# A third head's scores moved ahead of the value product, one split sum of two lanes, and two tile chains put around a value sum

## The chip, the cores and the metric

The kernel runs on one core of one Trainium2 chip. The metric is the device time of the run in microseconds, the median of several runs. Engines are named as in the profile: PE multiplies matrices (PEld is its weight load), DVE, ACT and POOL work on vectors, SP issues DMAs; POOL and ACT can issue DMAs too.

## The reference

A gated mix of two branches over the same x (2048 rows of 512): attention with 32 heads of 16 within a sliding window of 256, and a SwiGLU network with 1792 hidden columns.

```python
def _A_ref(x, wqkv, wo):
    B, S, D = x.shape
    H = 32; Dh = D // H; W = 256
    ...
    scores = jnp.einsum("bhqd,bhkd->bhqk", q, k) * (Dh ** -0.5)
    mask = (idx[:, None] - idx[None, :] >= 0) & (idx[:, None] - idx[None, :] < W)
    p = _softmax(jnp.where(mask[None, None], scores, -1e9), axis=-1)
    o = jnp.einsum("bhqk,bhkd->bhqd", p, v)
    return (lambda x, *d: x.transpose(*d))(o, 0, 2, 1, 3).reshape(B, S, D) @ wo
def _B_ref(x, w_gate, w_up, w_down):
    return (_silu(x @ w_gate) * (x @ w_up)) @ w_down
g = _sigmoid((x * gate_w).sum(-1, keepdims=True))
return g * _A_ref(x, A_wqkv, A_wo) + (1 - g) * _B_ref(x, B_w_gate, B_w_up, B_w_down)
```

## The kernel before

All of it is one program written out by hand: the order of the Python calls is the order of each engine's queue. There are three stages: a prologue (values, queries and keys, up to about 165 us), the attention stage (to about 637 us), and the network's second half with the output projections.

Matrices are split into a high and a low half of reduced precision (`split`), so that one product is three matmuls. In the attention stage most of the gate and up products of the network, one *sum* for each of 24 weights (`UNITS`) and four blocks of 512 rows, are made beside the attention. A sum has 3 x 4 = 12 products of 128 rows. The first weight's four sums are made with all 128 rows (`whole`); the others by `lanes`: each product is cut into its lower 64 rows (lane 0) and its upper 64 rows (lane 1). The two halves of the array work side by side, each on its own matmul. Both lanes add into one PSUM bank, so lane 1 must not begin a sum before lane 0 has ended it: it runs `LAG` = 18 steps behind, and its first matmul has a dependence on a later instruction of DVE or ACT (`BEHIND`). One `yield` of `lanes` is one *step*, a matmul of each lane. In the first 18 steps only lane 0 works, in the last 18 only lane 1.

The attention goes by groups of four heads (8 groups, `G`) and blocks of 128 rows (16). One *slot* t is one block of one group, and has four quarters (`hd`), of one head each. In a quarter the queue of PE gets:
- `stage1` (line 562): the scores of the next group's block, of whose masked maximum DVE takes care (line 564). They lie in a ring of three banks.
- `stage2` (line 601): the scores of this group with keys as rows; ACT takes the exponential (line 603) into `pt`, POOL masks it (lines 605 and 608). They lie in a ring of two banks (`pd`).
- some steps of `lanes`, by the table `DEAL`.

Heads 0 and 2 lie on the lower half of the rows, 1 and 3 on the upper; `stage2` takes the heads in the order 1, 0, 3, 2, so that the two scores of a quarter lie on opposite halves. In every fourth slot, behind the second quarter's steps, `av` (line 623) makes the value product of the four blocks before it: up to 96 small matmuls into two banks, of which the second is one of `pd`. `evacuate` empties them: ACT copies the second to `ob` (line 634), DVE copies the first (line 640, or adds both at once in the last group, line 636), and POOL sends the sum to `od`.

The last group (slots 112 to 127) has no `stage1`, and `stage2` is called for two heads at a time. Beside it two finished tiles of the network are made (`tile_early`: an exponential on ACT, then on DVE a sum, a reciprocal and two products, and a split), weights are loaded (`wd_early`, `wd_raw`), and the softmax denominators are inverted (`invert`). Functions put in `AT` by `at(k, ...)` and `later(n, ...)` are called at the end of quarter k. In slot 128 the last value product is made; the next stage's loads `got` (line 863) take the memory that the attention gives back.

Of the kernel before, what the change touches and what calls it, by code (L numbers as in the profile page):

```python
# [2 lines left out]

# [6 lines left out]
F32 = mybir.dt.float32  # L10
F32R = mybir.dt.float32r
AF = mybir.ActivationFunctionType
ALU = mybir.AluOpType
# [3 lines left out]
P = 128  # L17
S, D, H, DH, W, F = 2048, 512, 32, 16, 256, 1792
NK = D // P
NB = S // P  # L20
CH = 512
NCH = S // CH
# [11 lines left out]
def gated_mix(ctx, tc, xT, xn, wqk, wv, wo, wgu, wd, gw, out):  # L34
# [4 lines left out]
    nc = tc.nc  # L39
# [3 lines left out]
    dram = ctx.enter_context(tc.tile_pool(name="dram", bufs=1, space=DRAM))  # L43
# [3 lines left out]
    vd = dram.tile([G, P, NB, VW], F32, name="vd")  # L47
    od = dram.tile([G, P, S], F32, name="od")
    raws = dram.tile([NF, 2, NCH, P, CH], F32, name="raws")
    rd = dram.tile([NCH, H, CH], F32, name="rd")  # L50
    xd = [[dram.tile([2, P, 2 * CH], F32, name=f"xd{g}{hf}") for hf in range(2)] for g in range(G)]

# [33 lines left out]
    def run(gen, n=None):  # L86

        while n is None or n > 0:
            if next(gen, run) is run:
                break  # L90
            n = n and n - 1
# [14 lines left out]
    UNITS = [("f", f, i) for f in range(NSF, NF) for i in range(2)]  # L106
# [4 lines left out]
    def bank(n):  # L111
        names = BANKS[n if isinstance(n, str) else ("pa", "pb", "pc", "pd")[n]]
        names.append(names.pop(0))
        return psum.tile([P, CH], F32, name=names[-1])
# [98 lines left out]
    first = [bank(n // 2) for n in range(4)]  # L213
# [18 lines left out]
    def op_sums(raw):  # L232
        a11, a12, a21, a22 = (raw[:, i] for i in range(4))
        s = wide.tile([P, 4, 2 * P], F32, name="s")
        for o, in0, in1, op in ((1, a21, a22, ALU.add), (2, a11, a21, ALU.subtract),
                                (0, s[:, 1], a11, ALU.subtract), (3, a12, s[:, 0], ALU.subtract)):
            nc.vector.tensor_tensor(out=s[:, o], in0=in0, in1=in1, op=op)
        return s.rearrange("p a n -> p (a n)")
# [27 lines left out]
    for b in range(4, NB):  # L266
        ps = bank((b // 4 % 2) * 2 + b % 4 // 2)
# [21 lines left out]
            split(hi, lo, raw, nc.scalar, nc.gpsimd)  # L289
        return halves  # L290

    WKEYS, PEND = list(UNITS), []

    def prefetch():
        if WKEYS:
# [120 lines left out]
    for p in range(NP):  # L416
# [4 lines left out]
        for i, (n, a) in enumerate(order):  # L421
            product(p, n, a)
            if not last:
                if i == 4:
                    OP["a"] = op_a(RW[p + 1])
                if i == 5:
                    sums = op_sums(RW[p + 1])
# [39 lines left out]
    with ExitStack() as A:  # L467
# [4 lines left out]
        def kept():  # L472
            return sm.tile([P, CH], F32, name="ev", bufs=EV)

        BEHIND, AT, NOW = [], {}, [0]
# [3 lines left out]
        def later(n, *fs):  # L479
            AT.setdefault(NOW[0] + n, []).extend(fs)  # L480

        def at(k, *fs):
            AT.setdefault(k, []).extend(fs)
# [8 lines left out]
        def products(key, c):  # L492
            wh, wl = WT[key]
            return [(wt[:, k], xt[c][:, k]) for k in range(NK) for wt, xt in ((wh, xhi), (wh, xlo), (wl, xhi))]

        def copy_out(key, c, ps):
            place = kept()
            queue = nc.gpsimd if key == UNITS[-1] else nc.sync
            later(0, lambda: nc.scalar.copy(place, ps))
            later(3, lambda: queue.dma_start(raws[key[1], key[2], c], place))  # L500
# [7 lines left out]
                        copy_out(key, c, ps)  # L508
                    yield

        LAG = 3 * NK + 6

        def lanes():


            sums = [(key, c) for key in UNITS[1:] for c in range(NCH)]
            ps, turned = {}, {}
            for n in range(len(sums) * 3 * NK + LAG):
                for lane in range(2):
                    o, i = divmod(n - lane * LAG, 3 * NK)  # L520
                    if not 0 <= o < len(sums):
                        continue
                    if not lane and i == 0:
                        ps[o] = bank("pa")
                    w, x = products(*sums[o])[i]
                    r = slice(64 * lane, 64 * lane + 64)
                    mm = nc.tensor.matmul(ps[o], w[r], x[r], start=not lane and i == 0,  # L527
                                          stop=bool(lane) and i == 3 * NK - 1)
                    if lane and i == 0:
                        tc.add_manual_dep(mm.ins, BEHIND[turned.pop(o)].ins.name, SYNC, reason="the other rows are summed")  # L530
                    if i == 3 * NK - 1:
                        if lane:
                            copy_out(*sums[o], ps.pop(o))
                            if sums[o][1] == NCH - 1:
                                later(3, prepare)
                        else:
                            turned[o] = len(BEHIND)
                yield

        def stream():  # L540
# [9 lines left out]
        def stage1(g, qb):  # L550

            hf, b = divmod(qb, NB // 2)
            if b == 0:
                MX[g, hf] = sm.tile([P, 4, NB // 2], F32, name="mx")
            q0, k0 = qb * P, max(0, qb - 2) * P
            n = q0 + P - k0
            for hd in range(4):
                pr, j = divmod(hd, 2)
                r = slice(64 * j, 64 * j + 63)

                ps = bank("pd") if g == 0 and pr else bank("pc")
                nc.tensor.matmul(ps[:, :n], QT[g % 2][pr][r, q0:q0 + P], KT[g % 2][pr][r, k0:k0 + n],  # L562
                                 start=True, stop=True)
                mx = nc.vector.tensor_tensor_reduce(out=ps[:, :n], in0=ps[:, :n], in1=mask[:, 3 * P - n:],  # L564
                                                    scale=1.0, scalar=NEG, op0=ALU.add, op1=ALU.max,
                                                    accum_out=MX[g, hf][:, hd, b:b + 1])
                if g == 0:
                    BEHIND.append(mx)
                yield
# [43 lines left out]
        def av(g, c):  # L613

            AV[g, c] = bank("pc"), bank("pc" if g == G - 1 or g == G - 2 and c == NCH - 1 else "pd")

            orders = [[4 * c + m for m in ms if 4 * c + m >= 0] for ms in ((0, 1, 2, -1, -2, 3), (0, 1, -1, 2, 3, -2))]
            for n, kbs in enumerate(zip(*orders)):
                for j in range(4):
                    for h, (o, kb) in enumerate(zip(HALVES, kbs)):  # L620
                        k0 = kb * P + 64 * h
                        q0, q1 = max(k0, c * CH), min(k0 + W + 64, c * CH + CH)
                        nc.tensor.matmul(AV[g, c][h][32 * j:32 * j + 32, q0 - c * CH:q1 - c * CH],  # L623
                                         VG[4 * g + kb // 4][o, kb % 4, 17 * j:17 * j + 32],
                                         PT[g, kb, j // 2][o, j % 2, q0 - kb * P:q1 - kb * P],
                                         start=n == 0, stop=n == len(orders[0]) - 1, skip_group_check=True)
# [19 lines left out]
        first = chain(*(stage1(0, b) for b in range(NB)))  # L646
# [91 lines left out]
            wd_early(4 * (g7 + 1 + m) + 2, m, m)  # L738
        for n in range(2):
            at(4 * (g7 + 9) + 1 + n, lambda n=n: tile_load(n, RAW_AT[n]))  # L740
        for n, ticks in enumerate(((2, 5, 5, 5, 5, 10), (4, 8, 8, 8, 8, 14))):
            early = tile_early(n)
            for m in ticks:
                at(4 * (g7 + 10) + m, lambda early=early: run(early, 1))
# [10 lines left out]
            spread(4 * (16 * g + 9) + 3, 1, stack(g + 2, 0))  # L755
            spread(4 * (16 * g + 17) + 1, 1, stack(g + 2, 1))

        DEAL = [[[(hd + 1) * n // 4 - hd * n // 4 for hd in range(4)] for n in deal] for deal in ((4, 9, 9, 8), (9, 9, 9, 8))]
        DEAL[0][0] = 1, 2, 1, 0
        for t in range(G * NB + 1):  # L760
            g, i = divmod(t, NB)
            d, part = divmod(t, NSLOT)
            s1 = stage1(g + 1, i) if t < g7 else iter(())
            s2 = stage2(g, i) if t < G * NB else iter(())
            values = part == 0 and t > 0
            for hd in range(4):
                k = NOW[0] = NSLOT * t + hd
                run(s1, 1)
                if t < g7:
                    run(s2, 1)  # L770
                elif hd % 2 == 0:
                    run(s2, 2)
                if t == G * NB and hd == 0:
                    last_tile = tile_silu(2)
                    run(last_tile, 1)
                if t < G * NB:
                    run(steps, DEAL[t >= g7][part][hd])
                if hd == 1 and values:
                    av(*divmod(d - 1, NCH))
                    while UNDER:  # L780
                        UNDER.pop(0)()
                    evacuate(*divmod(d - 1, NCH))
                tick_end()
            if i in (7, 15) and g + 1 < G:
                UNDER.append(lambda g=g, i=i: put_max(g + 1, i // 8))
            if t >= 10 and t % 4 == 2 and t + 6 < G * NB:
                load_v((t + 6) // 4)
# [196 lines left out]
```

## Time and profile before

| | |
|---|---|
| median of 3 runs | 840.9 us (840.44 to 840.92) |
| the profiled execution | 843.89 us, span 842.2 us |
| PE busy | 830.5 us (99%) |
| PEld, DVE, ACT, POOL busy | 83%, 65%, 56%, 47% |
| DMA | 158.91 MB, 189 GB/s on the mean |
| mean granted clock of PE | 0.998 |

The profile is one execution; its time is above the median of the runs. Busy times count a matmul from its start to a modelled end, so that matmuls that overlap on the two halves of the array count once. In the timeline "x2" is two instructions of one group put together; a group in brackets is what ended the idle time before it. `64*128 64x512` is a matmul with 64 rows of weights and 512 columns.

### The profile page before, as it was taken

What the parts mean: (1) busy time and instruction counts of PE and PEld (TensorE: products, weight loads), DVE (VectorE), ACT (ScalarE), POOL (GpSimd) and SP (SyncE); (2) the same over time, 40 slices, a digit from 0 to 9 for tenths busy, and PEclk for the clock granted to TensorE, in tenths of its full rate; (3) what the DMA queues carried; (4) which work ended last, traced back from release to release, by engine and by line L of the source; (5) the groups of instructions that cost most, each with busy time, mean ns of one, the idle gap of its engine ahead of it and who ended that gap; (6) DMA issues with size and microseconds to landing.
All of it is one profiled execution on the core that took longest, in us unless ns stands there. A gap on an engine that the chain in (4) does not pass through costs nothing.

```text
span 842.2 us, 20499 instructions
## 1 busy us (share of the span) xinstructions
PE 830.5 (99%) x7681; PEld 700.5 (83%) x7681; DVE 548.5 (65%) x1424; ACT 471.3 (56%) x955; POOL 398.9 (47%) x713
## 2 busy tenths in 40 slices
PE   9999999999999999999999999999997999999997
PEld 7888888888888888888988888888775888888886
DVE  5675554258787887878878778675473647564652
ACT  7454553212576776766767667666674554434341
POOL 5124441440475665766666666666654115352220
PEclk9999999999999999999999999999999999999999
DMA  8456676484625656456654545533628899878611
GB/s 296 142 174 225 228 263 222 141 273 152 197 94 163 209 177 198 146 181 191 196 188 141 189 156 190 164 107 127 205 99 278 282 248 259 268 217 249 212 51 50
DMA packets 79843, 158.91 MB, mean 189 GB/s; under 512 B 14912, under 2 KB 19392, under 8 KB 79744
## 3 DMA queue, kind: packets, MB, share of 16 engines
q1 hardware_dynamic: 68256, 126.91, 46.7%
q0 software_dynamic: 10912, 29.65, 11.1%
q8 instruction: 60, 0.98, 0.5%
q10 hardware_dynamic: 576, 1.05, 0.4%
q14 instruction: 39, 0.32, 0.1%
HBM read 92.80 MB, written 64.75 MB: 187 GB/s over the span
## 4 chain that ended last, share of the span: by engine, by line
PE 96%; DMA 1%; POOL 1%; SPq 0%; ACT 0%; DVE 0%; issue 0%; DVEq 0%; ACTq 0%
PE pa L527 22%; PE pb L527 11%; PE pd L601 7%; PE pc L623 4%; PE pd L380 4%; PE pb L380 4%; PE pa L380 4%; PE pc L562 4%; PE pd L82 3%; PE pc L81 3%; PE pc L82 3%; PE pc L80 3%; PE pd L81 3%; PE pd L80 3%; PE pd L623 2%; PE pb L623 2%
## 5 line engine op out<-in xcount | busy, mean ns | idle before, releaser
L603 ACT ACTIVATE pt<-pd 128x384 f32<-128x384 f32 (+2 forms) x512 | 231.9, 474 | 50.8 <-PE pc L562 14.2
L564 DVE CUSTOM_DVE_ANT_0 pc<-pc,mask 128x384 f32<-128x384 f32 (+2 forms) x322 | 172.5, 547 | 33.6 <-PE pc L562 15.2
L601 PE MATMUL pd<-q,k 64*128 64x384 f32 (+2 forms) x512 | 175.1, 357 | 0.7 <-ACT ob L634 0.3
L527 PE MATMUL pa<-xlo,wh 64*128 64x512 f32 x496 | 161.8, 396 | 0.0
L527 PE MATMUL pa<-xhi,wl 64*128 64x512 f32 x496 | 160.2, 392 | 0.0
L527 PE MATMUL pa<-xhi,wh 64*128 64x512 f32 x496 | 159.4, 396 | 0.1
L605 POOL TENSOR_SCALAR_AFFINE_SELECT pt<-pt 128x256 f32<-128x256 f32 x256 | 111.5, 436 | 74.5 <-ACT pt L603 70.2
L601 PEld LDWEIGHTS pd<-q,k 64*128 64x128 f32 x512 | 92.5, 184 | 21.1 <-ACT ob L634 9.7
L562 PE MATMUL pc<-k,q 63*128 63x384 f32 (+2 forms) x322 | 105.9, 333 | 0.0
L527 PE MATMUL pb<-xlo,wh 64*128 64x512 f32 x240 | 94.8, 395 | 0.0
L527 PE MATMUL pb<-xhi,wh 64*128 64x512 f32 x240 | 94.6, 394 | 0.0
L527 PE MATMUL pb<-xhi,wl 64*128 64x512 f32 x240 | 94.2, 393 | 0.0
L564 DVE CUSTOM_DVE_ANT_0 pb<-pb,mask 128x384 f32<-128x384 f32 (+2 forms) x158 | 86.7, 549 | 11.0 <-PE pb L562 5.4
L608 POOL TENSOR_SCALAR_AFFINE_SELECT pt<-pt 128x256 f32<-128x256 f32 x224 | 92.4, 412 | 0.0
L527 PEld LDWEIGHTS pa<-xhi,wl 64*128 64x128 f32 x496 | 81.9, 185 | 1.7
L527 PEld LDWEIGHTS pa<-xhi,wh 64*128 64x128 f32 x496 | 79.9, 186 | 3.6 <-ACT pt L603 1.1
L527 PEld LDWEIGHTS pa<-xlo,wh 64*128 64x128 f32 x496 | 80.8, 185 | 1.3
L869 DVE TENSOR_TENSOR sg<-got,sg 128x512 f32<-128x512 f32 x53 | 41.8, 788 | 49.1 <-ACT sg L868 39.6
L564 DVE DVE_READ_ACCUMULATOR2_ANT mx<- 128x1 f32 x512 | 72.5, 142 | 0.0
L562 PEld LDWEIGHTS pc<-k,q 63*128 63x128 f32 x322 | 58.8, 184 | 7.3 <-issue 4.3
L623 PE MATMUL pd<-pt,vg 64*32 64x320 f32 (+4 forms) x1184 | 63.1, 346 | 0.0
L641 POOL TENSOR_TENSOR oe<-oe,ob 128x512 f32<-128x512 f32 (+1 forms) x28 | 35.0, 1251 | 55.0 <-ACT ob L634 50.9
(302 smaller groups left out, 2055.6 us busy)
## 6 DMA issues: line engine op xcount, KB each, us to landing
got<-raws SPq DMA_DIRECT2D x106, 256.0 KB
raws<-ev SPq DMA_DIRECT2D x92, 256.0 KB
q<-xd SPq DMA_DIRECT2D x96, 128.0 KB
k<-xd SPq DMA_DIRECT2D x96, 128.0 KB
xd<-cx SPq DMA_DIRECT2D x16, 512.0 KB
xd<-cy SPq DMA_DIRECT2D x16, 512.0 KB
od<-oe POOLq DMA_DIRECT2D x32, 256.0 KB, 3.2
raw<-wgu SPq DMA_DIRECT2D x24, 256.0 KB
```

The costliest lines, as they stand in the source:

```text
L80: nc.tensor.matmul(ps, lh, rh, start=start and i == 0, stop=False, skip_group_check=skip)
L81: nc.tensor.matmul(ps, lh, rl, start=False, stop=False, skip_group_check=skip)
L82: nc.tensor.matmul(ps, ll, rh, start=False, stop=stop and i == n - 1, skip_group_check=skip)
L380: nc.tensor.matmul(ps, l[:, w], r[:, k], start=n in (1, 2, 5) and k == m == 0, stop=k == 1 and m == 2, skip_group_check=True)
L527: mm = nc.tensor.matmul(ps[o], w[r], x[r], start=not lane and i == 0, stop=bool(lane) and i == 3 * NK - 1)
L562: nc.tensor.matmul(ps[:, :n], QT[g % 2][pr][r, q0:q0 + P], KT[g % 2][pr][r, k0:k0 + n], start=True, stop=True)
L564: mx = nc.vector.tensor_tensor_reduce(out=ps[:, :n], in0=ps[:, :n], in1=mask[:, 3 * P - n:], scale=1.0, scalar=NEG, op0=ALU.add, op1=ALU.m ...
L601: nc.tensor.matmul(ps[:, :n], KT[g % 2][pr][r, k0:k0 + P], QT[g % 2][pr][r, k0:k0 + n], start=True, stop=True)
L603: BEHIND.append(nc.scalar.activation(pt[:, j, :n], ps[:, :n], AF.Exp, scale=SCALE))
L605: nc.gpsimd.affine_select(out=pt[:, :, :P], in_=pt[:, :, :P], pattern=[[0, 2], [1, P]], compare_op=ALU.is_ge, fill=0.0, base=0, channel_mu ...
L608: nc.gpsimd.affine_select(out=pt[:, :, 2 * P:], in_=pt[:, :, 2 * P:], pattern=[[0, 2], [-1, P]], compare_op=ALU.is_ge, fill=0.0, base=-1, ...
L623: nc.tensor.matmul(AV[g, c][h][32 * j:32 * j + 32, q0 - c * CH:q1 - c * CH], VG[4 * g + kb // 4][o, kb % 4, 17 * j:17 * j + 32], PT[g, kb, ...
```

## The change

Three parts.

*The third head's scores.* In a slot with a value product, the `stage1` scores of the third quarter are issued in the second, ahead of `av`. The step of the third quarter is dealt to the fourth. This concerns the 27 slots 4, 8, ... 108.

```diff
-        DEAL[0][0] = 1, 2, 1, 0
+        DEAL[0][0] = 1, 2, 0, 1
...
-                run(s1, 1)
+                if not (values and hd == 2):
+                    run(s1, 1)
...
                 if hd == 1 and values:
+                    run(s1, 1)
                     av(*divmod(d - 1, NCH))
```

*One sum in two parts.* The second weight's fourth sum (`odd`) is taken out of the row. Lane 1 makes its upper half in the first 12 steps; ACT copies it out of PSUM and SP writes it to `spill`. Lane 0 makes its lower half at the very end, for which the weight is loaded and split a second time; the spilled half is loaded by POOL, DVE adds it, and POOL writes the sum. `lanes` has 1110 steps in place of 1122, and the last 16 slots get 8 steps each in place of 9, 9, 9 and 8.

```diff
-    WKEYS, PEND = list(UNITS), []
+    WKEYS, PEND = UNITS + [UNITS[1]], []
...
+            turn, sums = 3 * NK, [(key, c) for key in UNITS[1:] for c in range(NCH)]
+            odd = sums.pop(NCH - 1)
+            ps, turned = {odd: bank("pa")}, {}
+            rows = (sums + [odd], [odd] + [None] + sums)
+            starts = [[turn * o for o in range(len(sums) + 1)], [0, turn] + [turn * o + LAG for o in range(len(sums))]]
+
+            def odd_start(ps):
+                place = kept()
+                later(0, lambda: nc.scalar.copy(place, ps))
+                later(3, lambda: nc.sync.dma_start(spill, place))
+
+            def odd_end(ps):
+                place, rest = kept(), PART.pop()
+                later(0, lambda: nc.vector.tensor_tensor(out=place, in0=ps, in1=rest, op=ALU.add))
+                later(3, lambda: nc.gpsimd.dma_start(raws[odd[0][1], odd[0][2], odd[1]], place))
...
+                        if o is odd:
+                            PART.append(kept())
+                            nc.gpsimd.dma_start(PART[0], spill)
...
-        DEAL = [[[(hd + 1) * n // 4 - hd * n // 4 for hd in range(4)] for n in deal] for deal in ((4, 9, 9, 8), (9, 9, 9, 8))]
+        DEAL = [[[(hd + 1) * n // 4 - hd * n // 4 for hd in range(4)] for n in deal] for deal in ((4, 9, 9, 8), (8, 8, 8, 8))]
```

*Early tiles.* The steps of the two tiles' chains fall on other quarters, counted from slot 122; quarter 9 is the one in which slot 124's value product is made and summed, ahead of the tile's step.

```diff
-        for n, ticks in enumerate(((2, 5, 5, 5, 5, 10), (4, 8, 8, 8, 8, 14))):
+        for n, ticks in enumerate(((1, 3, 3, 3, 3, 12), (7, 9, 9, 9, 9, 15))):
```

How this moves the queues. First PE around a value product in the middle; before, with `stage1` on line 562, `stage2` on 601, steps on 527 and the product on 623:

```order
L527 MATMUL pa_3594<-xhi_96,wl 128x512
L527 MATMUL pa_3445<-xhi_92,wl 128x512
L623 MATMUL pb_3609<-pt,vg 32x320
...
L623 MATMUL pd_3610<-pt,vg 32x128
L562 MATMUL pc_3674<-k_1413,q_1387 128x384
L601 MATMUL pd_3678<-q_1513,k_1515 128x384
L527 MATMUL pa_3594<-xhi_96,wh 128x512
L527 MATMUL pa_3445<-xhi_92,wh 128x512
L562 MATMUL pc_3683<-k_1413,q_1387 128x384
L601 MATMUL pd_3686<-q_1513,k_1515 128x384
L562 MATMUL pb_3691<-k_1365,q_1345 128x384
```

and PE there after the change, where the lines are 595, 634, 556 and 656:

```order
L556 MATMUL pa_3611<-xhi_91,wl 128x512
L556 MATMUL pb_3468<-xhi_95,wl 128x512
L595 MATMUL pb_3626<-k_1414,q_1388 128x384
L656 MATMUL pc_3629<-pt,vg 32x320
...
L656 MATMUL pd_3630<-pt,vg 32x128
L634 MATMUL pd_3695<-q_1514,k_1516 128x384
L595 MATMUL pc_3698<-k_1414,q_1388 128x384
L634 MATMUL pd_3701<-q_1514,k_1516 128x384
L556 MATMUL pa_3611<-xhi_91,wh 128x512
L556 MATMUL pb_3468<-xhi_95,wh 128x512
L595 MATMUL pb_3708<-k_1366,q_1346 128x384
```

One score stands ahead of the product, and a step of two matmuls has gone behind the second `stage2` score.

DVE at the end of the attention stage, from the second tile's reciprocal on; before:

```order
L709 RECIPROCAL ev<-ev 128x512
L710 TENSOR_TENSOR ev<-q_1501,ev 128x512
L711 TENSOR_TENSOR ev<-q_1501,ev 128x512
L636 TENSOR_TENSOR oe<-pb_9988,ob 128x512
L71 TENSOR_TENSOR k_1503<-ev,k_1503 128x512
L457 RECIPROCAL den<-den 128x128
L71 TENSOR_TENSOR q_1513<-ev,q_1513 128x512
```

and after, from the sum of slot 124's product to the same places (the tile's chain is now lines 741 to 744):

```order
L669 TENSOR_TENSOR oe<-pb_9986,ob 128x512
L741 TENSOR_SCALAR ev<-ev 128x512
L742 RECIPROCAL ev<-ev 128x512
L743 TENSOR_TENSOR ev<-q_1502,ev 128x512
L744 TENSOR_TENSOR ev<-q_1502,ev 128x512
L458 RECIPROCAL den<-den 128x128
L72 TENSOR_TENSOR k_1504<-ev,k_1504 128x512
L72 TENSOR_TENSOR q_1514<-ev,q_1514 128x512
L530 TENSOR_TENSOR ev<-pb_10095,ev 128x512
```

The sum of slot 124's value product (`oe`) stood behind the second tile's chain and stands ahead of it now; the addition on line 530 is the split sum's.

POOL from the store of that product on; before:

```order
L642 DMA od<-oe 128x512
L500 DMA raws<-ev 128x512
...
L458 DMA rd<-den 128x128
...
L749 DMA raw<-wd 128x512
L749 DMA wh<-wd 128x512
L749 DMA wl<-wd 128x512
L500 DMA raws<-ev 128x512
L605 AFFINE_SELECT pt<-pt 128x2x128 x3
```

and after:

```order
L675 DMA od<-oe 128x512
...
L459 DMA rd<-den 128x128
...
L501 DMA raws<-ev 128x512
...
L553 DMA ev<-spill 128x512
L782 DMA raw<-wd 128x512
L782 DMA wh<-wd 128x512
L782 DMA wl<-wd 128x512
L638 AFFINE_SELECT pt<-pt 128x2x128 x2
```

The load of the spilled half stands ahead of the weight loads. `wh` and `wl` are memory of the ring that the lanes' weights use, and with one weight more in the ring it is the last weight's place that they take.

More of the change, by code (lines that the diff above doesn't have):

```diff
@@ L1 @@
 from contextlib import ExitStack
-from itertools import chain
+from itertools import chain, zip_longest
 import concourse.bass as bass
@@ L49, in gated_mix @@
     raws = dram.tile([NF, 2, NCH, P, CH], F32, name="raws")
+    spill = dram.tile([P, CH], F32, name="spill")
     rd = dram.tile([NCH, H, CH], F32, name="rd")
@@ L509, in whole, with items @@
                     yield
-        LAG = 3 * NK + 6
+        LAG, PART = 3 * NK + 6, []
         def lanes():
[L516 to L521, printed above, removed]
+            turn, sums = 3 * NK, [(key, c) for key in UNITS[1:] for c in range(NCH)]
[11 more added lines that the diff above has]
+                later(3, lambda: nc.gpsimd.dma_start(raws[odd[0][1], odd[0][2], odd[1]], place))
+            def items(lane):
+                for at_, o in zip(starts[lane], rows[lane]):
+                    while o and len(lines[lane]) < at_:
+                        lines[lane].append(None)
+                    if o:
+                        lines[lane].extend((o, i) for i in range(turn))
+            lines = [], []
+            items(0)
+            items(1)
+            for both in zip_longest(*lines):
+                for lane, item in enumerate(both):
+                    if item is None:
@@ L522, in lanes @@
                         continue
-                    if not lane and i == 0:
+                    o, i = item
+                    first = o is odd or not lane
+                    if first and i == 0 and not (lane and o is odd):
                         ps[o] = bank("pa")
-                    w, x = products(*sums[o])[i]
+                        if o is odd:
+                            PART.append(kept())
+                            nc.gpsimd.dma_start(PART[0], spill)
+                    w, x = products(*o)[i]
@@ L526, in lanes @@
                     r = slice(64 * lane, 64 * lane + 64)
-                    mm = nc.tensor.matmul(ps[o], w[r], x[r], start=not lane and i == 0,
-                                          stop=bool(lane) and i == 3 * NK - 1)
-                    if lane and i == 0:
+                    mm = nc.tensor.matmul(ps[o], w[r], x[r], start=first and i == 0,
+                                          stop=(o is odd or bool(lane)) and i == turn - 1)
+                    if not first and i == 0:
                         tc.add_manual_dep(mm.ins, BEHIND[turned.pop(o)].ins.name, SYNC, reason="the other rows are summed")
[L531 to L537, printed above, removed]
+                    if i < turn - 1:
+                        continue
@@ L538, in lanes @@
+                    if o is odd:
+                        (odd_start if lane else odd_end)(ps.pop(o))
+                    elif not lane:
+                        turned[o] = len(BEHIND)
+                    else:
+                        copy_out(*o, ps.pop(o))
+                        n = sums.index(o) + 1
+                        if n == len(sums) or sums[n][0] != o[0]:
+                            later(3, prepare)
                 yield
```

## The prediction

> **What bounds the kernel now.** I read the page first, for the engine shares and the chain that ended last, then what the weight loads of PE waited for, then the timeline around one value product, and last the timeline of the end of the attention stage.
>
> ```profile
> span 842.2 us, 20499 instructions
> PE 830.5 (99%) x7681; PEld 700.5 (83%) x7681; DVE 548.5 (65%) x1424; ACT 471.3 (56%) x955; POOL 398.9 (47%) x713
> PE 96%; DMA 1%; POOL 1%; SPq 0%; ACT 0%; DVE 0%; issue 0%; DVEq 0%; ACTq 0%
> PEld pd L601 <- ACT ob L634: 9.7, 27, 0.6
> ```
>
> PE is the chain, so whatever lengthens PE's own queue lengthens the kernel. But 99% busy is made of modelled ends: the weight loads stood idle 27 times for a copy of `ob`, which is once for each value product that still has stage 1 beside it. The other half of the price is in how two 64-row halves of the array share the time:
>
> ```profile
> 179.15 0.34 PE L562 MATMUL pc<-k,q 63*128 63x384 f32 x1
> 179.33 0.39 PE L527 MATMUL pa<-xhi,wh 64*128 64x512 f32 x1
> 179.56 0.39 PE L527 MATMUL pa<-xlo,wh 64*128 64x512 f32 x1
> 588.53 0.55 PE L527 MATMUL pa<-xhi,wh 64*128 64x512 f32 x2
> 588.77 0.55 PE L527 MATMUL pa<-xlo,wh 64*128 64x512 f32 x2
> ```
>
> At 179.33 one half works alone and a step of one matmul takes 0.23 us (179.33 to 179.56). At 588.53 both halves work and a step of two takes 0.24. A lone step costs what a paired one does. A 384-column score holds its half for 0.18 us (179.15 to 179.33).
>
> Here is one value product in the middle (slot 60, 384-column scores), PE and then ACT:
>
> ```profile
> 409.52 0.43 PE L527 MATMUL pa<-xhi,wl 64*128 64x512 f32 x2
> 409.88 0.45 PE L623 MATMUL pb<-pt,vg 64*32 64x320 f32 x1
> ...
> 412.25 0.27 PE L623 MATMUL pd<-pt,vg 64*32 64x128 f32 x1
> 412.45 0.44 PE L562 MATMUL pc<-k,q 63*128 63x384 f32 x1
> 412.45 0.43 PE L601 MATMUL pd<-q,k 64*128 64x384 f32 x1
> 412.73 0.39 PE L527 MATMUL pa<-xhi,wh 64*128 64x512 f32 x2
> 412.96 0.34 PE L562 MATMUL pc<-k,q 63*128 63x384 f32 x1
> 413.28 0.44 PE L601 MATMUL pd<-q,k 64*128 64x384 f32 x1
> 413.55 0.34 PE L562 MATMUL pb<-k,q 63*128 63x384 f32 x1
> 413.67 0.44 PE L601 MATMUL pd<-q,k 64*128 64x384 f32 x1
> ...
> 423.01 0.45 PE L623 MATMUL pc<-pt,vg 64*32 64x320 f32 x1
> ```
>
> ```profile
> 412.64 0.59 ACT L634 COPY ob<-pd 128x512 f32<-128x512 f32 x1 [2.33 <-PE pd L623]
> 413.12 0.50 ACT L603 ACTIVATE pt<-pd 128x384 f32<-128x384 f32 x1
> ```
>
> After the last value matmul (412.25) PE has three things that need nothing from ACT: the third head's pair of scores (412.45), a paired step (412.73), the fourth head's L562 (412.96). The fourth head's L601 must have the bank that ACT is emptying: `ob` is copied from 412.64 to 413.23, and PE goes on at 413.28. That instant, 1.03 us behind the last value matmul, is set by ACT, not by how much PE did meanwhile.
>
> **The change part by part.** *Third head first.* In 27 slots the third head's L562 moves ahead of the value product, and the step of that quarter moves to the fourth, behind its L601. The number of matmuls stays, so the question is what each covered.
>
> Ahead of the product the score uses the lower half alone: the next instruction is a value matmul on the lower half, and the upper one has nothing between. The product starts 0.36 us behind the last step (409.52 to 409.88), so that gap is a step of 0.24 and 0.12 of turning over; a score put between adds its 0.18. In six of the slots the score has 128 columns instead of 384, a third, so 0.06 (estimate). Sum: 21 x 0.18 + 6 x 0.06 = 4.1 us. What it leaves behind the product is a shorter list in the same wait: L601, the fourth head's L562, and then idleness until 1.03 as before, because ACT's copy starts from the product's end. So nothing is gained there.
>
> The step now stands behind that wait. The lower half, held by the fourth L601 until 413.55, would take it to about 413.78. The upper half was idle anyway until 413.67, where the next L601 waits for the first exponential behind the copy (413.12 plus 0.50), so there the step fills a hole. Between nothing (the upper half, which sets the next quarter, loses nothing) and a whole step of 0.23 a slot, 0 to 6.2 us; below nothing is excluded, since the release does not move and no less work is left behind it. I take 0.06 a slot, near the low end, as the upper half is the later one in the rows: 1.6 us. The move costs 5.7 us, with ends of 4.1 and 10.3.
>
> A rule on the halves speaks the other way. The Trainium skill's "TensorEngine Tiling (Array Packing)", Key Properties, says that different tiles load and multiply in parallel, but that changing the tiling mode drains the array. By its first half the score would cost nothing beside the product's upper half; by its second it costs its full time. The gap of 0.36 against a pace of 0.24 agrees with the second.
>
> DVE also does that head's masked maximum earlier, while it waits for the product; nobody on PE waits for it in these slots.
>
> *The sum put aside.* The two lanes lay 18 steps apart, so 18 steps were lone at either end. Twelve at each end are now paired with the split sum, and 12 steps leave the run: 12 x 0.23 = 2.8 us of PE. It adds a copy on ACT, two DMAs of 256 KB, one more weight split (ACT and POOL) and an addition on DVE. They run on engines that are 35% to 53% idle beside a PE that is 99% busy, so I cost them at nothing; uncovered, a copy of this size is 0.59. The saved steps leave the last 16 slots, nine of them before the product of slot 124: that product ends 9 x 0.23 = 2.1 us earlier. What comes of it is settled by the third part.
>
> *Early tiles.* Rows of the end of attention, DVE, ACT, POOL, PE:
>
> ```profile
> 621.59 0.42 DVE L708 TENSOR_SCALAR ev<-ev 128x512 f32<-128x512 f32 x1
> 626.77 0.68 DVE L636 TENSOR_TENSOR oe<-pb,ob 128x512 f32<-128x512 f32 x1
> 627.97 0.95 DVE L457 RECIPROCAL den<-den 128x128 f32<-128x128 f32 x1
> ```
>
> ```profile
> 622.30 0.59 ACT L634 COPY ob<-pc 128x512 f32<-128x512 f32 x1 [2.73 <-PE pc L623]
> 626.88 0.62 ACT L68 CAST q<-ev 128x512 fp32r<-128x512 f32 x1 [0.37 <-DVE ev L711]
> ```
>
> ```profile
> 627.75 0.56 POOL L642 DMA_DIRECT2D od<-oe  x1 [7.34 <-DVE oe L636]
> 630.04 0.56 POOL L458 DMA_DIRECT2D rd<-den  x1
> 632.03 0.56 POOL L749 DMA_DIRECT2D raw<-wd  x1
> 634.20 1.30 POOL L605 TENSOR_SCALAR_AFFINE_SELECT pt<-pt 128x256 f32<-128x256 f32 x3
> 636.03 0.42 POOL L605 TENSOR_SCALAR_AFFINE_SELECT pt<-pt 128x256 f32<-128x256 f32 x1
> ```
>
> ```profile
> 630.84 0.39 PE L527 MATMUL pa<-xhi,wl 64*128 64x512 f32 x1
> ...
> 634.84 0.40 PE L623 MATMUL pc<-pt,vg 64*32 64x256 f32 x1 [1.96 <-POOL pt L605]
> SPq L863 <- PE pb L623: 15.0, 1, 15.0
> ```
>
> Now both tiles' chains stand ahead of the sum `oe`, so POOL sits 7.34 us at `od<-oe`. After the change the first chain runs earlier, the sum comes as soon as `ob` is there, and the second chain behind it. With the product 2.1 earlier, `ob` is ready at 622.89 - 2.1 = 620.8, the sum ends at 621.5, and the chain, 5.2 us (621.59 to 626.77), at 626.7. The cast of the second tile waits on ACT for that chain as it does now (626.88); behind it are queued the exponentials of the last two slots, whose banks PE needs. Eleven of the 12 steps lie ahead of that point, so PE gets there 11 x 0.23 = 2.5 us earlier and the cast 0.2 earlier: PE waits 2.3 us longer in slot 126, and its stream (last step now at 630.84) ends only 2.8 - 2.3 = 0.5 earlier. That is where most of the 2.8 goes.
>
> POOL is free of `od` at 622, but its next row `rd<-den` waits for the small reciprocal behind the second chain: 627.9 instead of 630.04. Behind it are the same masks, stores and weight loads, plus the load of the spilled sum, 0.56 (as 632.03). The `wh` load, which stands behind the `raw` load, now has to wait for the last step of the stream, 630.3, but POOL comes to it only at about 631.6 (632.03 + 0.56 - 2.1, the spill load, and a store that moves ahead of it). So the last mask starts at 636.03 - 2.1 + 0.6 = 634.5, 1.5 us earlier. The first loads of the next stage wait for the last value matmul (the SP row), and PE runs three finished tiles meanwhile, so the stage should follow: I take 1.5 us, with ends of 0 (the loads come no earlier, since a store more is in their way) and 2.8 (all 12 steps).
>
> **Sum.** 5.7 - 1.5 = 4.2 us more. The profiled execution took 843.9 us in all, of which 842.2 are the span; by its own time the changed kernel is at 848.1. The median of the runs is 840.9, 3.0 lower, and the same 4.2 on it makes 845.1. The bounds alone: 4.1 - 2.8 = 1.3 and 10.3 - 0 = 10.3, but the parts will hardly all meet their ends; the case's own range is 842.7 to 848.0.
>
> **The rivals.** *Faster: the moved score is free.* If a lower-half score runs while the array turns over for the product, or beside the product's upper half, the 27 slots cost nothing, and the end gives 1.5 to 2.8: 838.1 to 839.4, say 838.7. For it: 0.12 us of the gap before the product is no matmul. Against it: the gap is the same where the neighbours are lighter, and a 0.18 score does not fit in 0.12 unless the two overlap wholly. It decides below 0.05 us a slot. Chance 0.16.
>
> *Even.* The score half hides (0.08 x 27 = 2.2) and the end gives 2.2 to 2.8: 840.3 to 840.9. Chance 0.14.
>
> *Slower still: the new hole lowers PE's clock.* The trace has one such case:
>
> ```profile
> 645.00:648.00 3.00, 1.15 (x4) 0.30 (x2) 0.77 (x2) 1.84 (x4) 1.59 (x3) 1.00 1.04 401
> 648.00:652.00 4.00, 3.42 (x9) 2.70 (x10) 2.94 (x5) 2.67 (x6) 0.00 (x0) 0.57 1.00 320
> ```
>
> With PE busy 1.15 of 3 us at the start of the next stage the granted clock fell to 0.57 for the next 4: 4 x 0.43 = 1.7 us lost. The wait of 2.3 us in slot 126 may do the same to the last steps, which `wh` on POOL then waits for: 845.1 + 1.7 = 846.8, and with the step at 0.12 a slot 848.4. The Trainium skill's "TensorE: Matmul & The Clock Gate", Part 1, halves the clock after an idle window of about 3.4 us whose start is free; by it a hole of 2.3 us would not be enough. The 1.96 us hole at 634.84 did not lower it: it still reads 1.00 at 645. Chance 0.11.
>
> That leaves 0.59 for the forecast.
>
> **How the numbers follow.** About 0.2%, 1.7 us, is what a measurement of this kernel tells from no change. Slower by more: 0.59 + 0.11 = 0.70. Within: 0.14. Faster: 0.16. The range 839.3 to 848.2 leaves out most of the first rival and the tail of the last, about 0.15 to 0.2.
>
> **What would show it.** Right: in the slots of the value products the gap from the last step to the first value matmul reads 0.36 + 0.18; the fourth L601 still comes 1.03 us behind the last value matmul, now with a longer wait for `ob`; from one product to the next is 13.4 us where it is 13.1 (409.88 to 423.01); POOL's 7.34 is gone, and PE has a hole of some 2.3 us behind the cast of the second tile. Wrong: a gap that stays at 0.36 (the score is free), a fourth L601 that comes sooner (the release was not ACT's alone), or a stream that ends 2.8 us earlier without the hole.

## The result, and the profile after

The changed kernel takes 842.81 us (median of 12 runs, 842.17 to 846.21), the kernel before 840.74 in the same comparison (12 runs, 839.57 to 841.86). The ratio is 1.0029, 95% interval 1.0019 to 1.0039: slower by 2.1 us. Its profiled execution is the longest of its 12 runs, 846.21 us, so the sections below compare places in the trace and not its total.

The page of the changed kernel (span, busy times, chain) and, from its waits, the rows for the bank of `ob`:

```profile
span 844.5 us, 20512 instructions
PE 824.5 (98%) x7681; PEld 692.8 (82%) x7681; DVE 552.2 (65%) x1425; ACT 472.8 (56%) x956; POOL 402.5 (48%) x716
PE 91%; POOL 2%; ACT 2%; issue 2%; DMA 1%; SPq 0%; DVE 0%; ACTq 0%; DVEq 0%; POOLq 0%
PEld pd L634 <- ACT ob L667: 14.8, 27, 0.8
```

PE is busy for less time (830.5 to 824.5 us), and the wait for `ob`, 27 times as before, went from 9.7 to 14.8 us. The two belong together, but they are not the loss: `a_deal` below has both without it. The value product of slot 60, PE then ACT:

```profile
411.79 0.39 PE L556 MATMUL pa<-xhi,wl 64*128 64x512 f32 x1
411.80 0.39 PE L556 MATMUL pb<-xhi,wl 64*128 64x512 f32 x1
412.03 0.33 PE L595 MATMUL pb<-k,q 63*128 63x384 f32 x1
412.29 0.45 PE L656 MATMUL pc<-pt,vg 64*32 64x320 f32 x1
412.30 0.45 PE L656 MATMUL pd<-pt,vg 64*32 64x320 f32 x1
...
414.58 0.27 PE L656 MATMUL pd<-pt,vg 64*32 64x128 f32 x1
414.78 0.44 PE L634 MATMUL pd<-q,k 64*128 64x384 f32 x1
415.06 0.34 PE L595 MATMUL pc<-k,q 63*128 63x384 f32 x1
415.60 0.44 PE L634 MATMUL pd<-q,k 64*128 64x384 f32 x1 [0.21 <-ACT ob L667]
415.61 0.49 PE L556 MATMUL pa<-xhi,wh 64*128 64x512 f32 x1
415.89 0.39 PE L556 MATMUL pb<-xhi,wh 64*128 64x512 f32 x1
```

```profile
414.96 0.59 ACT L667 COPY ob<-pd 128x512 f32<-128x512 f32 x1 [2.42 <-PE pd L656]
```

The lone score at 412.03 lies between the last step and the product: 0.50 us (411.79 to 412.29) where it was 0.36. Behind the product the fourth head's L634 still comes 1.02 us after the last value matmul (414.58 to 415.60), and PE now stands idle 0.21 us ahead of it. That is the shorter list in the same wait: the step now stands behind it.

What 27 such slots cost is read from the first value matmul of the first product to that of slot 112, before and after:

```profile
228.06 0.45 PE L623 MATMUL pc<-pt,vg 64*32 64x320 f32 x1
...
579.54 0.45 PE L623 MATMUL pb<-pt,vg 64*32 64x320 f32 x1
```

```profile
228.40 0.45 PE L656 MATMUL pb<-pt,vg 64*32 64x320 f32 x1
...
582.66 0.45 PE L656 MATMUL pb<-pt,vg 64*32 64x320 f32 x1
```

351.48 us became 354.26: 2.8 us, 0.10 a slot. The end of the attention stage, DVE, ACT, POOL and PE of the changed kernel:

```profile
621.46 0.78 DVE L744 TENSOR_TENSOR ev<-k,ev 128x512 f32<-128x512 f32 x1
624.53 0.69 DVE L669 TENSOR_TENSOR oe<-pb,ob 128x512 f32<-128x512 f32 x1 [2.30 <-ACT ob L667]
625.14 0.42 DVE L741 TENSOR_SCALAR ev<-ev 128x512 f32<-128x512 f32 x1
...
630.31 0.94 DVE L458 RECIPROCAL den<-den 128x128 f32<-128x128 f32 x1
```

```profile
630.43 0.62 ACT L69 CAST q<-ev 128x512 fp32r<-128x512 f32 x1 [2.62 <-DVE ev L744]
```

```profile
625.52 0.56 POOL L675 DMA_DIRECT2D od<-oe  x1 [2.54 <-ACT pt L636]
...
631.55 0.56 POOL L459 DMA_DIRECT2D rd<-den  x1 [4.69 <-ACT pt L636]
...
634.46 0.56 POOL L553 DMA_DIRECT2D ev<-spill  x1
...
637.91 1.23 POOL L638 TENSOR_SCALAR_AFFINE_SELECT pt<-pt 128x256 f32<-128x256 f32 x2
```

```profile
631.38 0.66 PE L634 MATMUL pd<-q,k 64*128 64x256 f32 x2 [2.21 <-ACT pt L636]
...
634.06 0.39 PE L556 MATMUL pa<-xhi,wl 64*128 64x512 f32 x1
...
637.10 0.40 PE L656 MATMUL pc<-pt,vg 64*32 64x256 f32 x1 [1.40 <-POOL pt L638]
```

The sum `oe` no longer stands behind the second chain, and of POOL's 7.34 us at `od` 2.54 are left. But the chain, put behind the sum, ends at 630.4; the cast waits for it on ACT with exponentials behind it, and PE has a hole of 2.21 us. The stream's last step comes at 634.06 (630.84 before), though slot 112 was only 3.1 later and 12 steps are gone. POOL waits 4.69 us at `rd<-den`, with the last masks behind it (the bracket names an exponential, but the store needs the reciprocal of `den`, which ends at 631.25), so the product waits in its middle for a mask at 637.10.

### The profile page after: what moved, and what is told of

Read it like the earlier page. It is cut to its first block, busy times and chain, and to the rows that moved or that the text cites. A ratio compares the mean times of both kernels' runs of the same rounds, so it can differ in the third digit from the quotient of the medians.

```text
span 844.5 us, 20512 instructions
## 1 busy us (share of the span) xinstructions
PE 824.5 (98%) x7681; PEld 692.8 (82%) x7681; DVE 552.2 (65%) x1425; ACT 472.8 (56%) x956; POOL 402.5 (48%) x716
## 4 chain that ended last, share of the span: by engine, by line
PE 91%; POOL 2%; ACT 2%; issue 2%; DMA 1%; SPq 0%; DVE 0%; ACTq 0%; DVEq 0%; POOLq 0%
PE pa L556 20%; PE pb L556 10%; PE pd L634 6%; PE pc L656 4%; PE pd L381 4%; PE pb L381 4%; PE pa L381 4%; PE pd L83 3%; PE pc L595 3%; PE pc L83 3%; PE pc L82 3%; PE pc L81 3%; PE pd L82 3%; PE pd L81 3%; PE pb L656 2%
## 5 line engine op out<-in xcount | busy, mean ns | idle before, releaser
L634 PE MATMUL pd<-q,k 64*128 64x384 f32 (+2 forms) x512 | 174.1, 352 | 9.5 <-ACT ob L667 6.8
L556 PE MATMUL pa<-xhi,wl 64*128 64x512 f32 x492 | 157.7, 393 | 0.0
L556 PE MATMUL pa<-xlo,wh 64*128 64x512 f32 x492 | 157.4, 393 | 0.0
L634 PEld LDWEIGHTS pd<-q,k 64*128 64x128 f32 x512 | 93.2, 184 | 35.2 <-ACT ob L667 14.8
L595 PE MATMUL pc<-k,q 63*128 63x384 f32 (+2 forms) x322 | 103.2, 327 | 0.0
L556 PE MATMUL pb<-xhi,wh 64*128 64x512 f32 x244 | 97.1, 398 | 0.0
L556 PEld LDWEIGHTS pa<-xhi,wl 64*128 64x128 f32 x492 | 79.6, 185 | 1.7
L904 DVE TENSOR_TENSOR sg<-got,sg 128x512 f32<-128x512 f32 x53 | 45.4, 857 | 46.2 <-ACT sg L903 38.7
```

The source lines that it names most:

```text
L556: mm = nc.tensor.matmul(ps[o], w[r], x[r], start=first and i == 0, stop=(o is odd or bool(lane)) and i == turn - 1)
L634: nc.tensor.matmul(ps[:, :n], KT[g % 2][pr][r, k0:k0 + P], QT[g % 2][pr][r, k0:k0 + n], start=True, stop=True)
```

## The experiments

Each kernel is timed in five rounds against the kernel before on its chip, whose median is given in brackets.

**The first part alone, the second alone, the third alone, and the last two together.** `a_only` is the kernel before with this:

```diff
+        DEAL[0][0] = 1, 2, 0, 1
-                run(s1, 1)
+                if not (values and hd == 2):
+                    run(s1, 1)
                 if hd == 1 and values:
+                    run(s1, 1)
```

> The kernel before with the first part alone (third head's score ahead of the value product, its step dealt to the fourth quarter). Theory: the score holds the lower half of PE ahead of the product and leaves a shorter list in the wait for ob; the trace of the whole change shows slot 112 reached 3.1 us later. So 3.0 us more, 843.7, and the end of the stage as it is now, only shifted. Rival: the shift is given back, because the end of the stage waits for POOL anyway: within 0.8 us of before. Second rival: the shift came from the split sum's extra copies, not from this part: within 0.5 us, and slot 112 not later.

Measured: 843.63 us (841.22), ratio 1.0033 [1.0015, 1.0051], 2.4 us more. The first part alone makes the whole loss and costs under half of the 5.7 forecast.

`b_only` is the kernel before with the split sum (the new `lanes`) and

```diff
-for deal in ((4, 9, 9, 8), (9, 9, 9, 8))]
+for deal in ((4, 9, 9, 8), (8, 8, 8, 8))]
```

> The kernel before with the split sum alone (12 steps fewer, 8 in each of the last 16 slots, spill and reload), the tiles' chains on their old quarters. Theory: seven steps leave ahead of the chains, which start 1.6 us earlier, and everything behind them (cast, POOL's masks) follows by that: 1.6 us less, 839.2. Rival: all 12 steps come off, 2.8 us less, 838.0. Second rival: the wh load on POOL, which now waits for the stream's end, and the spill load hold the masks back: no gain or up to 1 us more.

Measured: 840.38 us (841.22), ratio 0.9997 [0.9984, 1.001]: not to be told from no change, where 12 steps of 0.23 us had left PE. Its profile, of an execution of 842.82 us, 2.4 above the median, shows a wait of PE for an exponential, 1.13 us (PE row), a stretch at half clock behind it (windows of 3 us: busy time of PE, PEld, DVE, ACT and POOL, then the granted clock, DMA share and GB/s), and on POOL `od` still waiting behind both chains:

```profile
624.46 1.07 PE L634 MATMUL pd<-q,k 64*128 64x384 f32 x2 [1.13 <-ACT pt L636]
```

```profile
622.00:625.00 3.00, 1.87 (x13) 1.25 (x12) 2.93 (x4) 1.88 (x5) 0.00 (x0) 0.98 0.52 165
625.00:628.00 3.00, 3.00 (x16) 3.00 (x18) 2.93 (x4) 0.98 (x2) 0.00 (x0) 0.50 0.03 10
```

```profile
628.95 0.56 POOL L675 DMA_DIRECT2D od<-oe  x1 [9.35 <-ACT q L69]
```

`c_only` is the kernel before with the new ticks:

```diff
-((2, 5, 5, 5, 5, 10), (4, 8, 8, 8, 8, 14))
+((1, 3, 3, 3, 3, 12), (7, 9, 9, 9, 9, 15))
```

> The kernel before with the tiles' chains moved alone. Theory: the second chain runs behind the value sum of slot 124 and ends some 2 us later than now (628.9 in place of 626.9); the second tile's cast on ACT waits for it with the last exponentials behind it, so PE gets a hole of about 2 us in slot 126; POOL's store of the small reciprocal is as late as now. Since the last product waits for POOL's masks anyway, 0 to 0.5 us more, 840.9 to 841.4. Rival: POOL's 7.3 us behind the store of the sum were the cost, and 1 to 2 us come off.

Measured: 842.62 us (841.22), ratio 1.0022 [1.001, 1.0034], worse than expected. The hole is there, and PE's clock fell behind it (PE row, then windows); the mean granted clock is 0.993 to 0.996 in all 12 runs:

```profile
629.34 0.76 PE L527 MATMUL pa<-xhi,wh 64*128 64x512 f32 x1 [2.30 <-ACT pt L603]
```

```profile
626.00:629.00 3.00, 1.04 (x6) 0.51 (x5) 2.93 (x4) 0.64 (x3) 0.00 (x0) 1.00 0.00 0
629.00:640.00 11.00, 10.66 (x115) 7.08 (x116) 2.26 (x4) 5.13 (x14) 6.55 (x14) 0.53 0.38 127
```

`bc` is the changed kernel without the first part:

```diff
-        DEAL[0][0] = 1, 2, 0, 1
+        DEAL[0][0] = 1, 2, 1, 0
-                if not (values and hd == 2):
-                    run(s1, 1)
+                run(s1, 1)
                 if hd == 1 and values:
-                    run(s1, 1)
```

> The whole change without its first part. Theory: the whole change (2.1 us more) less the 3.0 of the first part: 0.9 us less than before, 840.0, with slot 112 reached at the same time as before and the hole in slot 126 still there. Rival: the first part costs nothing on the clock, and this stays 2 us above before.

Measured: 840.46 us (841.22), ratio 0.9992 [0.9976, 1.0008]. The second and third parts together give some 0.7 us, and not surely that: the interval goes from 2.0 us less to 0.7 more.

**The first part taken apart.** `a_score` moves the score and leaves the step; `a_deal` moves the step and leaves the score.

```diff
 a_score
-                run(s1, 1)
+                if not (values and hd == 2):
+                    run(s1, 1)
                 if hd == 1 and values:
+                    run(s1, 1)
 a_deal
-        DEAL[0][0] = 1, 2, 1, 0
+        DEAL[0][0] = 1, 2, 0, 1
```

> The kernel before with the third head's score ahead of the value product, but its step left in the third quarter, in the wait for ob. Theory: the cost is the score's lone time ahead of the product; the step's place costs nothing, because the upper half waits for the next exponential anyway. So as much as the first part whole: 3.0 us more, 843.7. Rival: the cost is the step that lost its cover: then this is within 0.8 us of before, and the move of the step carries the rest.

> The kernel before with only the step moved from the third quarter to the fourth, behind the score that waits for ob; the third head's score stays behind the product. Theory: within 0.8 us of before (the step fills the hole of the upper half). Rival: 0.1 to 0.2 us for each of 27 slots, 2.7 to 5.4 us more.

Measured: `a_score` 843.25 us (840.72), ratio 1.0033 [1.0021, 1.0046], 2.5 us; `a_deal` 841.15 us, ratio 1.0003 [0.9994, 1.0013]. The loss is the score's; the step's place costs nothing that can be told. The traces agree: from the first value matmul of the first product to that of slot 112 it is 353.89 us in `a_score` and 351.55 in `a_deal`, against 351.48 before. The longer wait for `ob` goes with the step and not with the loss (`a_deal`, then `a_score`):

```profile
PEld pd L601 <- ACT ob L634: 14.4, 27, 0.8
PEld pd L601 <- ACT ob L634: 10.1, 27, 0.6
```

PE's busy time is 822.1 us in `a_deal` and 830.1 in `a_score`. A step inside the wait makes PE look busier and the wait look shorter, and changes nothing of when the bank comes free.

**What holds the end of attention.** `bc_late` is `bc` with the second tile's split (its cast on ACT) eight quarters later. `bc_fix` also clears POOL's queue ahead of the last masks: the second inversion (with `rd<-den`) goes from the end of slot 124 into slot 128, and the loads of `wh` and `wl` two slots on.

```diff
 bc_late
-((1, 3, 3, 3, 3, 12), (7, 9, 9, 9, 9, 15))
+((1, 3, 3, 3, 3, 12), (7, 9, 9, 9, 9, 23))
 bc_fix, besides
-at(4 * (g7 + 5 + 4 * c) + 3 + 12 * n, ...)
+at(4 * (g7 + 5 + 4 * c) + 3 + (12 + 13 * c) * n, ...)
-((13, "raw"), (13, "wh"), (13, "wl"), (17, "wh"), (17, "wl"))
+((13, "raw"), (15, "wh"), (15, "wl"), (17, "wh"), (17, "wl"))
```

> The split sum and the moved chains, without the first part, and the second tile's split (cast on ACT) put from quarter 15 to 23, behind the last exponentials. Theory: the 2.2 us hole in slot 126 goes and the stream ends 2 us earlier, but the masks on POOL still wait for the small reciprocal behind the second chain and for the stream's end (wh), so the last product ends no more than 0.5 us earlier than with the cast in its place: 839.5 to 840.0. Rival: the hole was the whole loss, and this is 2 us faster than with the cast in its place, 838.

> As the one with the late cast, and also POOL's queue cleared for the last masks: the second inversion of denominators goes to slot 128, the wh and wl loads that wait for the stream's end go behind the last masks. Theory: the last value product then follows the stream's end without a wait, some 4 us earlier than with POOL in the way (it needs 2.4 us in place of 5.1 to 5.6); the next stage's loads come as much earlier: 836.5 to 838 us. Rival: the next stage waits for its own data, so that what is gained ahead is idle behind it: 839 to 840.

Measured: `bc_late` 840.05 us (840.72), ratio 0.9992 [0.9981, 1.0003]; `bc_fix` 833.98 us, ratio 0.9924 [0.9911, 0.9938]. In `bc_late` the hole is gone and the stream ends 4.9 us sooner than in `bc` (628.36, against 633.28, where the hole and the half clock behind it both count), and the time is the same within the intervals. Its POOL rows say why: the masks still stand behind `rd<-den`, the spilled sum and the weight loads.

```profile
628.55 0.56 POOL L459 DMA_DIRECT2D rd<-den  x1 [4.69 <-ACT pt L636]
...
631.10 0.56 POOL L553 DMA_DIRECT2D ev<-spill  x1
631.66 0.54 POOL L782 DMA_DIRECT2D raw<-wd  x1
632.19 0.54 POOL L782 DMA_DIRECT2D wh<-wd  x1
632.72 0.54 POOL L782 DMA_DIRECT2D wl<-wd  x1
...
634.55 1.23 POOL L638 TENSOR_SCALAR_AFFINE_SELECT pt<-pt 128x256 f32<-128x256 f32 x2
```

In `bc_fix` the last masks come ahead of these loads (POOL), and from 625 to 640 PE is busy 14.47 of 15 us at full clock (window):

```profile
628.97 0.77 POOL L638 TENSOR_SCALAR_AFFINE_SELECT pt<-pt 128x256 f32<-128x256 f32 x2
629.68 0.55 POOL L782 DMA_DIRECT2D wh<-wd  x1
```

```profile
625.00:640.00 15.00, 14.47 (x161) 11.32 (x160) 9.81 (x15) 9.60 (x20) 9.51 (x18) 1.00 0.78 285
```

From its first value matmul to its last the product takes 2.3 us (5.1 in the changed kernel); the last one starts at 630.88, where it was 636.76 before. Of the gaps at the start of the next stage (1.58 and 0.85 us before) one of 0.53 is left. It is more than the theory gave, and beats both kernels. Beside `bc_late`, from which only the two moves in POOL's queue part it, `bc_fix` is 6.1 us faster. Which of the two does it no run tells.

**The two parts with that queue cleared.** `fix_only` has `bc_fix`'s ticks, inversion and loads on the kernel before, with its whole sums; `after_fix` has them on the changed kernel, with its moved score.

```diff
 both
-at(4 * (g7 + 5 + 4 * c) + 3 + 12 * n, ...)
+at(4 * (g7 + 5 + 4 * c) + 3 + (12 + 13 * c) * n, ...)
-(13, "wh"), (13, "wl")
+(15, "wh"), (15, "wl")
+((1, 3, 3, 3, 3, 12), (7, 9, 9, 9, 9, 23))
```

> The whole sums of before (no split, 9 steps in the last slots) with the cleared queue of POOL and the late cast: how much of the 6.7 us is the queue's and how much the 12 steps'. Theory: PE now sets the end of the stage, so 12 steps of 0.23 us are worth their whole 2.8 us: 834.0 + 2.8 = 836.8, last step at about 631.0 in the profile, last product's end at about 633.7 (628.27 and 630.88 with the split sum). Rival: the steps lie beside waits for ACT that are as long without them, so they are worth nothing even now: 834.0 to 834.6. Second rival: the queue still is behind, and clearing it alone gives little: over 838.

> The changed kernel whole, its third head's scores ahead too, with the same cleared queue and late cast. Theory: the moved score costs the 2.4 to 3.1 us of the runs before on PE, which is the chain up to the end here: 836.4 to 837.1. Rival: part of what the score cost in the changed kernel came from where the end of attention fell against POOL's queue, and with the queue clear it costs under 1.5: below 835.5. Second rival: it costs the 5.7 us that were forecast: 839.7.

Measured: `fix_only` 836.42 us (840.57), ratio 0.9946 [0.9932, 0.9959]; `after_fix` 836.9 us, ratio 0.9951 [0.9939, 0.9963]. Beside `bc_fix` (0.9924), the split sum is worth 1.8 to 2.4 us (by the ratios and by the medians) once PE sets the end of the stage, and the moved score costs 2.3 to 2.9 there as elsewhere; each ratio is good to about 1 us. On the whole sums the moved chains, the late cast and the cleared queue together give 4.2 us; there they were not taken apart.

## Why the prediction was right, and where it missed

The forecast was +4.2 us; +2.1 was measured, with the sign and the mechanism as put, and both terms too large: the cost by about 3 us, the gain by about 1. The two errors go opposite ways, so the sum came nearer than its larger term, and that is luck.

*"The move costs 5.7 us, with ends of 4.1 and 10.3."* It costs 2.3 to 2.9 (`a_only`, `a_score`, `after_fix` beside `bc_fix`), under the lower end. Two sizes failed.

The score: 0.18 in each wide slot. Ahead of the product that is right. From the second matmul of the last step to the first value matmul it is 0.32 or 0.33 us in each of the 27 slots before, and after the change 0.49 or 0.50 in the 21 wide ones and 0.38 or 0.39 in the six narrow ones (PE rows of both profiles). That is 4.0 us in all, where the forecast had 4.1. What the forecast left out is that the product itself became shorter. Before, in 14 of the 27 products, the second bank's first matmul comes 0.09 to 0.14 us behind the first bank's; in slot 60 it is 0.10, behind 409.88 (PE):

```profile
409.98 0.45 PE L623 MATMUL pd<-pt,vg 64*32 64x320 f32 x1
```

Now the two start together in all 27 (412.29 and 412.30 in slot 60), and those 14 products are 0.08 to 0.13 us shorter from the first value matmul to the last. So 1.3 of the 4.0 us came back inside the products, and 2.8 are left, 0.10 a slot. `a_score` has the same gaps (to 0.02) and the same products, so this too comes with the score's place; why the second bank was late before stays open. By the Trainium skill's "TensorEngine Tiling (Array Packing)", Key Properties, a change of mode drains the array; a gap that grew by 0.17 for a score of 0.18 agrees with this.

The step: 0.06 a slot for its place behind the wait. `a_deal` gives 0.03%, with an interval from -0.06% to 0.13%. The rows show the reason that the forecast gave for the upper half: its one half starts at 415.61, beside L634 at 415.60, in time that stood empty.

The release stayed at 1.02 us, as forecast, with a longer wait for `ob`.

*"From one product to the next is 13.4 us where it is 13.1."* In that pair it is 12.87 (412.29 to 425.16):

```profile
425.16 0.45 PE L656 MATMUL pb<-pt,vg 64*32 64x320 f32 x1
```

One pair was a poor sign. Of the seven pairs of the same kind, from the third product of a group to its fourth, three took 12.87 or 12.88 already before (358.00 to 370.88 is one), and four 13.13 to 13.19, as the one picked. Only the sum over all 27 shows the cost.

*The stream and the hole.* The hole of some 2.3 us behind the cast is there: 2.21. The 7.34 us of POOL went down to 2.54. The stream was to end 0.5 us earlier; counted from slot 112 it ends 0.1 later (634.06 less 3.12, against 630.84). Nine steps were to save 2.1 us ahead of slot 124's product. From the first score of slot 112 to that of slot 124 it is 39.99 us before (578.15 to 618.14) and 38.44 after (581.27 to 619.71), so 1.55: the terms of 0.23 a step assume that PE waits for nothing else there. It does: in that stretch the weight loads of the scores waited 2.6 us in 12 waits for exponentials before, and 4.7 in 19 after (waits of PEld). So part of what the steps gave back went into these waits.

*"The last mask starts 1.5 us earlier."* The last value matmul starts at 639.45 where it was 636.76, and slot 112 is 3.1 later: the end gained 0.4 and not 1.5. Two sizes make the difference. `rd<-den` comes at 631.55, where 627.9 and the 3.1 make 631.0: 0.55 late, with the sum, as the nine steps saved 0.55 less. From there to the last mask the forecast had 6.6 us (627.9 to 634.5); it took 7.1 to 7.2, as the last two masks end at 639.14 (637.91 and 1.23) and one takes about 0.4. `bc` measures these two parts without the first: 0.7 us, not to be told from nothing. The step of the sum that failed here is the 1.5; `bc_late` and `bc_fix` show that at full clock POOL's queue, and not PE's stream, ends the stage.

*Even, as a rival,* had the score nearer than the forecast, 0.08 a slot where 0.10 was measured; what it had wrong is the end, which it put at 2.2 to 2.8 us.

*The clock as a rival* came true in part. In the profile of the changed kernel the hole left the clock at 1.00 (window):

```profile
631.00:634.00 3.00, 2.62 (x19) 2.35 (x20) 1.61 (x3) 2.11 (x9) 2.42 (x5) 1.00 0.06 22
```

But behind a hole of 2.30 us it fell in `c_only`, and behind one of 2.21 in `bc` (PE row, then window):

```profile
628.56 0.85 PE L634 MATMUL pd<-q,k 64*128 64x256 f32 x2 [2.21 <-ACT pt L636]
```

```profile
628.00:639.00 11.00, 10.44 (x118) 7.16 (x119) 3.17 (x5) 5.76 (x15) 7.58 (x16) 0.53 0.49 174
```

Of the changed kernel's 12 runs, nine have a mean granted clock of 0.993 to 0.996, where the profiled one has 0.997: by this the clock was down for longer in most of them, though without a profile not where. These nine took 842.37 to 843.68 us, their median 842.86; the two at 0.999 and 1.0 took 842.17 and 842.31. So, as far as two runs tell, the slow stretch costs about 0.6 us in the changed kernel, and not 1.7 on top. Two profiles suggest why so little: in `bc`, at half clock, PE waits for no mask in its last product, and in `bc_late`, without the hole, it waits four times for POOL's masks, 3.3 us in all. The slow stretch takes up time in which PE would else stand idle. For the changed kernel's other runs this is argued.

## What to carry to other kernels

Work that leaves the busiest engine saves time only where that engine ends the stage: here 12 steps gave nothing measurable until two loads and one small inversion were taken out of the way of the last masks, and then about 2 us. Moving a piece of work ahead of a wait that is timed by another engine gains nothing behind it and costs what it does not overlap in front. How long an engine waits, or how busy it looks, does not tell the cost: here the run with the longer wait lost nothing, and the run with the loss had nearly the old wait. And a wait should be followed to the next one in line before its end is booked as a gain: POOL went from a wait of 7.34 us to one of 4.69 with the same masks behind it.

## What the runs showed of the hardware

PE's granted clock may or may not halve behind a hole of about 2.2 us: it did behind 2.30 and 2.21 us in two profiles, not behind 2.21 in a third, and in `b_only` it did behind a wait of 1.13. The stretch that followed was also of two lengths, some 3 us in `b_only` and some 10 us in `c_only` and `bc`, though PE's records show it busy all the while. What decides this, no run here shows. The Trainium skill's "TensorE: Matmul & The Clock Gate", Part 1, has about 3.4 us for either change, with windows whose start is free. The free start agrees with a hole that strikes in one profile and not in another; holes under 3.4 us that strike, and a recovery of 10, do not.
